# Cutting the first W1 load by contraction tile, issuing the first M and MLP matmuls as separate operations and rewriting every engine's order list, in a fused attention and MLP kernel

## Chip, cores, metric

One core of one Trainium2 chip. The metric is device time in microseconds (us) of the slowest core, here the only one. The profile's span of the same execution is 1.8 us shorter. A change counts as faster or slower at 2 per cent.

## The reference

```python
def _attn_ref(q, k, v):                       # (8, 8, 576, 64) each
    q_s = softmax of q over its last axis
    k_s = softmax of k over the sequence
    kv = einsum('bhsd,bhse->bhde', k_s, v)
    return einsum('bhsd,bhde->bhse', q_s, kv)

def _moe_ref(x, w_in, w_out):                 # (4608, 512), (512, 2048), (2048, 512)
    h = x @ w_in
    g = where(h > 0, h, exp(minimum(h, 0)) - 1)
    return g @ w_out
# the output is _moe_ref(heads of the attention side by side, w_in, w_out)
```

(The two softmaxes are shortened to words.)

## The kernel before

The 4608 tokens go through the MLP in 9 blocks of 512. A block has 8 groups; a group is 8 matmuls of the first layer (two tiles of 128 columns of W1, four contraction tiles each), an ELU on ACT and DVE, and then its share of the second layer's 64 matmuls. The attention is done in units ("pairs") of four heads of one batch, and each pair gives two of the four contraction tiles (of 128 rows) of XT, the MLP's input, for the 576 tokens of its batch; one tile holds two of its heads. Pair 0 gives tiles 0 and 1, with which the MLP starts; pair 1 gives tiles 2 and 3, needed a little later. In what follows, q, k and v are the loaded inputs; qsT is the softmaxed q, transposed; VB is v cast to bf16; "kv" are the matmuls of k with v, whose scaled result stands in MBLK; "M" are the matmuls of MBLK with qsT that give XT; GT is the ELU's output, the second layer's input; PS is PSUM. Each engine's operations follow a list that was written down by number (`ORDER`), and waits on semaphores are derived from what each operation reads and writes.

```python
CH = 9; NU = 16                      # pieces of a unit; units ("pairs" below)

def load_w1(self, g0, g1, half, key, after=()):   # half 0: contraction tiles 0, 1; half 1: 2, 3
    ...
    for h in range(2):               # the two halves of the partitions
        self.S.add("gp", ..., lambda e, h=h: e.dma_start(self.W1[h:128:2, ks, sl], w[h, :, ks, sl]), ...)

def ao_mm(self, n, x, ps, at=0):     # "M": XT of a pair = its block-diagonal M times its qsT
    def mm(e):
        for f in range(2):           # two matmuls, two PSUM banks, one operation
            last = e.matmul(P[:, y:y + n_], M[:, f, :], T[:, c0:c1, f * 64:f * 64 + 64], ...)

def hg_mm(self, j, g, ps, key, half=None):        # first layer, group g of block j
    def mm(e):
        for t in range(2):
            for kc in kcs:           # all four contraction tiles, or two of them
                last = e.matmul(P[:, t * 512:(t + 1) * 512], self.W1[:, kc, ...], self.XT[:, kc, ...], ...)

# start of the program (cut)
for g0, g1, half in ((0, 3, 0), (0, 3, 1), (3, 5, None), (5, 8, None)):
    self.load_w1(g0, g1, half, -30, ...)
...
self.load_w2(0, -29); self.load_w2(1, -29)        # W2 comes in four quarters, between q, k, v of pairs 2 and 3
...
for half in range(2):                             # groups 0 to 2 of block 0
    for g in range(3):
        self.hg_mm(0, g, turns[g], key, half)
for g in range(8):
    self.hg(0, g, turns[g], key, "da"[g % 2], g > 2)
```

The softmax here doesn't subtract the row's maximum and nothing guards it: scores larger than these inputs give would overflow.

Of the kernel before, what the change touches and what calls it, by code (L numbers as in the profile page):

```python
# [21 lines left out]
ISSUE = {"sp": 550, "act": 550, "gp": 740}  # L22
ORDER = {
    "pe": (
        "30 28 32 43 45 47 50 67 54 68 70 71 69 72 82 86 93 115 103 90 129 128 137 136 131 139 107 "
        "130 138 109 151 152 150 126 134 149 132 156 157 158 140 173 146 153 159 172 174 175 233 238 "
        "237 239 192 243 249 245 244 251 250 201 255 257 256 203 263 262 212 268 261 267 269 313 309 "
        "321 317 350 220 325 333 329 280 391 334 282 338 342 291 412 346 351 299 399 404 395 417 362 "
        "400 364 408 425 430 373 413 421 438 426 381 479 434 439 487 450 500 492 483 505 488 452 513 "
        "518 461 496 469 501 526 509 564 514 572 522 538 585 527 540 568 577 573 598 581 586 590 594 "  # L30
        "603 611 549 607 636 599 556 657 640 612 662 644 649 653 645 670 622 666 624 683 688 658 679 "
        "632 675 671 634 696 709 684 692 701 714 697 705 722 727 735 718 710 740 731 748 723 744 761 "
        "736 766 757 753 749 770 787 762 774 779 775 783 788 792 793 805 797 801 809 "),
    "act": (
        "3 22 33 23 24 31 29 34 35 48 44 55 73 76 77 79 83 84 87 94 95 97 104 91 92 116 117 119 98 "
        "108 120 127 135 133 163 160 179 147 166 154 169 205 176 230 231 188 234 180 240 241 191 246 "
        "215 252 253 202 258 204 211 264 213 265 273 270 214 218 310 322 314 217 284 318 221 279 326 "
        "294 355 281 330 296 335 283 290 392 343 297 292 339 293 347 366 352 376 300 405 361 396 378 "
        "363 401 409 365 372 418 375 443 414 454 379 422 374 431 427 382 464 435 449 480 440 451 466 "
        "493 467 484 531 489 453 460 463 506 519 462 497 470 502 542 510 515 565 537 523 539 554 551 "  # L40
        "528 569 578 574 541 552 616 582 591 587 595 548 555 550 608 637 600 626 557 604 641 613 650 "
        "654 621 646 623 663 667 689 631 625 659 680 633 676 672 685 693 715 702 698 635 706 719 728 "
        "711 732 741 724 745 737 767 758 750 771 754 763 776 780 784 789 794 798 806 802 810 812 "),
    "dve": (
        "2 4 5 0 6 7 25 26 37 27 38 39 40 41 42 36 46 49 51 52 53 56 74 75 78 80 81 85 88 89 96 100 "
        "105 106 101 102 122 118 110 111 112 123 124 141 142 143 148 155 182 183 184 177 178 232 206 "
        "235 236 193 194 207 195 196 197 242 208 247 198 248 254 259 260 266 274 275 271 272 276 311 "
        "312 285 319 222 223 286 320 224 225 226 227 287 327 328 356 331 332 357 336 337 358 344 345 "
        "348 349 367 353 368 354 301 369 302 303 304 305 306 397 398 402 403 410 411 444 415 416 445 "
        "446 423 424 428 429 383 384 455 385 386 387 388 436 456 457 437 441 442 485 490 486 532 491 "  # L50
        "498 499 533 471 503 472 534 473 474 504 511 543 544 512 475 476 516 517 524 525 545 529 530 "
        "570 571 575 576 583 584 596 597 617 588 618 589 609 610 601 558 602 619 642 643 559 627 560 "
        "561 562 614 615 628 629 563 655 656 647 648 668 669 660 661 673 674 681 682 686 687 694 695 "
        "707 699 708 700 720 721 712 713 733 734 725 726 746 747 738 739 759 760 751 752 772 764 765 "
        "773 777 778 785 786 "),
    "gp": (
        "1 14 15 16 17 18 19 20 21 57 59 58 63 60 61 62 64 66 99 65 113 125 144 121 114 145 181 186 "
        "189 "),
    "sp": (
        "8 9 10 11 12 13 170 187 161 164 171 185 165 190 200 168 162 199 209 210 216 167 219 277 278 "  # L60
        "229 228 323 315 288 295 316 289 324 298 341 359 308 360 377 307 340 393 370 371 406 394 420 "
        "380 407 419 447 433 390 465 482 432 458 448 389 494 481 495 459 468 478 507 520 535 477 567 "
        "508 521 536 553 566 546 580 547 579 620 605 638 606 593 592 630 651 652 639 677 665 690 664 "
        "678 703 716 717 691 730 704 729 756 768 769 742 755 743 782 781 790 791 795 796 799 800 807 "
        "808 803 804 811 "),
}


# [14 lines left out]
class Sched:  # L83
# [17 lines left out]

    def add(self, eng, dur, emit, key, R=(), W=(), X=(), dma=None, nbytes=0, after=(),
            follow=None, side=0):
# [136 lines left out]
def t_f32r(n):  # L240
    return (n + 32) / 2.4


class Gen:
# [82 lines left out]
            return (self.VR1, "vR1") if n in (1, 3) else (self.VR, "vR0")  # L327
        return self.RAW[n % 2][t], f"{t}R{n % 2}"

    def load_w1(self, g0, g1, half, key, after=()):  # L330
        w = self.w_in.rearrange("(h kc d) f -> h d kc f", h=2, d=D)
        sl = slice(g0 * 256, g1 * 256)
        ks = slice(0, 4) if half is None else slice(2 * half, 2 * half + 2)
        xs = (0, 1) if half is None else (half,)
        for h in range(2):
            self.S.add("gp", ISSUE["gp"], lambda e, h=h: e.dma_start(
                self.W1[h:128:2, ks, sl], w[h, :, ks, sl]), key,
                W=[f"W1_{g}{x}{h}" for x in xs for g in range(g0, g1)],
                dma=f"w1{g0}{xs[0]}{h}", nbytes=(len(xs) * (g1 - g0) << 17) * (1.25 if g0 == 3 else 1), after=after,
                follow=self.gpq)  # L340
            self.gpq = self.S.ops[-1]

    def load_w2(self, s, key, after=()):
        w = self.w_out.rearrange("(jj p) c -> p jj c", p=128)
# [105 lines left out]
    def kv_mm(self, n, ps, at=KV):  # L450
        i = n % 2
        P, ek, VB = self.PS[ps], self.ek(i), self.VB[i]

        def mm(e):
            for c in range(CH):
                for f in range(2):
                    for h in range(2):
                        fs, hs = slice(f * 64, f * 64 + 64), slice(h * 64, h * 64 + 64)
                        x = f * 512 + at
                        last = e.matmul(P[hs, x:x + D + 1], ek[fs, h, c, :],  # L460
                                        VB[fs, h, c, 0:D + 1], start=(c == 0), stop=(c == CH - 1))
            return last
        return 615 if at == self.KV else 290, [f"kR{i}", f"VB{i}", f"VB{i}x", f"VBone{i}"], mm

    def m(self, n, ps, key, at=KV):
        S, i, rz = self.S, n % 2, self.RZK[n % 2]
# [15 lines left out]
    def ao_mm(self, n, x, ps, at=0):  # L482
        i = n % 2
        P, M, T = self.PS[ps], self.MBLK[i], self.qsT[self.alt(n)]
        c0, c1 = self.part(n, x)
        n_ = (c1 - c0) * 64

        def mm(e):
            for f in range(2):
                y = f * 512 + at  # L490
                last = e.matmul(P[:, y:y + n_], M[:, f, :],  # L491
                                T[:, c0:c1, f * 64:f * 64 + 64], start=True, stop=True)
            return last
        return (2 * t_f32r(n_), [f"qsT{self.alt(n)}{y}" for y in (0, 1)] +
                [f"MBLK{i}{y}" for y in ("", 0, 1)], mm)

    def xt(self, n, x, ps, key, eng="act", at=0):
        S = self.S
# [32 lines left out]
            names += [(f"Ox{i}{x}", at, at + 2048) for x in range(2)]  # L531
        return [n for n, lo, hi in names if lo < 4096 * (g + 1) and hi > 4096 * g]

    def hg_mm(self, j, g, ps, key, half=None):
        S = self.S
        P = self.PS[ps]
        banks = [f"b{2 * ps}", f"b{2 * ps + 1}"]
        rc = BLK * (j % 3)
        kcs = range(4) if half is None else range(2 * half, 2 * half + 2)
        xs = [f"X{kc}_{(8 * j + x) % (RING // 64)}" for kc in kcs for x in range(8)]  # L540
        ws = [f"W1_{g}{x}{h}" for x in sorted({kc // 2 for kc in kcs}) for h in range(2)]

        def mm(e):
            for t in range(2):
# [94 lines left out]
    def program(self):  # L639
# [4 lines left out]
        for n, t in ((0, "q"), (1, "q"), (0, "k"), (0, "v"), (1, "k"), (1, "v")):  # L644
            self.load(n, t, -40, "sp", follow=self.gpq)
            self.gpq = S.ops[-1]
            if (n, t) == (0, "k"):
                gate = S.ops[-1]
        loaded = S.ops[-1]
        for g0, g1, half in ((0, 3, 0), (0, 3, 1), (3, 5, None), (5, 8, None)):  # L650
            self.load_w1(g0, g1, half, -30, [gate, self.ident] if half == 0 else ())
            S.ops[-2].behind = loaded
        AB, C, D_ = 3, 2, 1
        self.stage1(0, -8, vconv=CAST0)
# [2 lines left out]
        self.stage1(1, -5, vconv=CAST1)  # L657
        self.m(0, C, -12)
        self.tp(1, D_, -7, ("act", "dve"))
        self.side(C, -5, self.ao_mm(0, 0, C))  # L660
        self.xt(0, 0, C, -10, "both")
        self.side(0, -3, self.kv_mm(1, 0))
        kv1 = S.ops[-1]
        self.m(1, 0, -12)
        S.spare_until = S.ops[-4]
        self.side(0, -2, self.ao_mm(1, 0, 0))
        self.xt(1, 0, 0, -10, "both")
        for o in S.ops:
            if o.eng == "pe":
# [4 lines left out]
            start=True, stop=True)  # L674
# [89 lines left out]

        key = 0
        turns = [3, 1, 2, 0, 3, 1, 0, 2]
        for half in range(2):
            for g in range(3):
                self.hg_mm(0, g, turns[g], key, half)
        for g in range(8):  # L770
            self.hg(0, g, turns[g], key, "da"[g % 2], g > 2)
            if g == 4:
# [50 lines left out]
        i = self.oslot % len(self.OSB)  # L823
# [43 lines left out]
```

## Time and profile before

| | before |
|---|---|
| time, median of 3 runs, later of 6 | 301.47, 301.38 us |
| span of the profiled execution | 299.0 us |
| PE busy | 96% |
| first MLP matmul | 14.95 us |
| last W1 columns landed | 24.71 us |
| last MLP matmul starts | 295.72 us |

PE is the bound, so it is read as one stream. Here are its two main groups of instructions, from the page: line, engine, operation, tiles, shapes and count, then the time busy, the mean ns of one, and the idle time ahead of them.

```profile
L592 PE MATMUL PS<-W,GT 128*128 128x512 f32 (+1 forms) x592 | 141.4, 386 | 0.4 <-DVE GT L582 0.4
L547 PE MATMUL PS<-XT,W 128*128 128x512 f32 x576 | 140.5, 391 | 0.7 <-DVE RZK L469 0.5
```

The two MLP layers have 592 and 576 matmuls and keep PE for 282 of 299 us. The idle time shown is short, but it isn't the whole of what a wait costs: a matmul counts as busy until its modelled end, so a pause shows in full only in the distance between the starts of two matmuls. When nothing waits, that distance is 227 ns. Below I count the 1168 MLP matmuls by their starts and compare the time of the same one in two kernels. This "lag" shows where in the program time is won and lost.

### The profile page before, as it was taken

What the parts mean: (1) busy time and instruction counts of PE and PEld (TensorE: products, weight loads), DVE (VectorE), ACT (ScalarE), POOL (GpSimd) and SP (SyncE); (2) the same over time, 40 slices, a digit from 0 to 9 for tenths busy, and PEclk for the clock granted to TensorE, in tenths of its full rate; (3) what the DMA queues carried; (4) which work ended last, traced back from release to release, by engine and by line L of the source; (5) the groups of instructions that cost most, each with busy time, mean ns of one, the idle gap of its engine ahead of it and who ended that gap; (6) DMA issues with size and microseconds to landing.
All of it is one profiled execution on the core that took longest, in us unless ns stands there. A gap on an engine that the chain in (4) does not pass through costs nothing.

```text
span 299.0 us, 4421 instructions
## 1 busy us (share of the span) xinstructions
PE 287.1 (96%) x1851; PEld 234.5 (78%) x1851; DVE 189.5 (63%) x244; ACT 182.3 (61%) x212; POOL 21.7 (7%) x33
## 2 busy tenths in 40 slices
PE   0899999999999999999999999999999999999995
PEld 0487877677888888888888888888888888888885
DVE  3958935985898685894568855588427256655500
ACT  5858848988977967867755766534462423432411
POOL 0860145100000000000000000000000000000000
PEclk9999999999999999999999999999999999999999
DMA  7999998994498697289546327041312302004214
GB/s 260 387 398 389 390 391 262 240 371 157 118 247 259 141 338 181 71 263 266 175 116 164 88 66 186 2 99 37 86 36 51 70 2 53 0 0 107 64 41 105
DMA packets 35443, 49.96 MB, mean 167 GB/s; under 512 B 16352, under 2 KB 16608, under 8 KB 35424
## 3 DMA queue, kind: packets, MB, share of 16 engines
q1 hardware_dynamic: 29840, 34.15, 41.3%
q0 software_dynamic: 5504, 15.47, 16.3%
q8 instruction: 14, 0.23, 0.3%
q10 hardware_dynamic: 80, 0.07, 0.1%
q14 instruction: 5, 0.04, 0.1%
HBM read 36.70 MB, written 9.44 MB: 154 GB/s over the span
## 4 chain that ended last, share of the span: by engine, by line
PE 89%; DVE 4%; DMA 3%; ACT 1%; SPq 1%; issue 0%
PE PS L592 43%; PE PS L547 41%; PE PS L491 3%; DMA QT<-QS 2%; PE PS L460 2%; DMA QR<-in_q_dram 1%; DVE ZQ L376 1%; DVE QS L384 1%; PE PS L407 1%; SPq L634 1%; DVE XT L516 0%; DVE GT L582 0%; ACT QR L356 0%; ACT qsT L435 0%; ACT ESB L563 0%; DVE MBLK L473 0%
## 5 line engine op out<-in xcount | busy, mean ns | idle before, releaser
L592 PE MATMUL PS<-W,GT 128*128 128x512 f32 (+1 forms) x592 | 141.4, 386 | 0.4 <-DVE GT L582 0.4
L547 PE MATMUL PS<-XT,W 128*128 128x512 f32 x576 | 140.5, 391 | 0.7 <-DVE RZK L469 0.5
L547 PEld LDWEIGHTS PS<-XT,W 128*128 128x128 f32 x576 | 107.1, 188 | 24.0 <-DVE XT L516 0.9
L592 PEld LDWEIGHTS PS<-W,GT 128*128 128x128 f32 x592 | 107.7, 188 | 22.1 <-DVE GT L582 0.8
L563 ACT ACTIVATE ESB<-PS 128x1024 f32<-128x1024 f32 x72 | 73.7, 1027 | 64.7 <-PE PS L547 64.3
L580 DVE TENSOR_SCALAR ESB<-ESB 128x1024 f32<-128x1024 f32 x64 | 44.4, 695 | 67.0 <-ACT ESB L563 66.4
L582 DVE TENSOR_TENSOR GT<-ESB,PS 128x1024 fp32r<-128x1024 f32 x64 | 77.7, 1217 | 1.8
L624 ACT ACTIVATE OSB<-PS 128x512 f32<-128x512 f32 x31 | 18.2, 598 | 30.9 <-PE PS L592 30.6
L376 DVE TENSOR_REDUCE ZQ<-QR 128x18 f32<-128x1152 f32 x16 | 21.5, 1344 | 7.3 <-ACT QR L356 7.2
L513 ACT ACTIVATE XT<-PS 128x512 fp32r<-128x512 f32 (+6 forms) x32 | 19.5, 608 | 7.0 <-PE PS L491 6.5
L384 DVE TENSOR_TENSOR QS<-QR,RZQ 128x1152 f16<-128x1152 f32 x16 | 21.6, 1353 | 0.3
L356 ACT ACTIVATE QR<-QR 128x1152 f32<-128x1152 f32 x16 | 18.6, 1165 | 2.9 <-DMA QR<-in_q_dram 2.9
L360 ACT ACTIVATE KR<-KR 128x1152 bf16<-128x1152 f32 x16 | 18.5, 1160 | 3.0 <-DMA KR<-in_k_dram 3.0
L435 ACT ACTIVATE qsT<-QT 128x1152 fp32r<-128x1152 f16 x12 | 14.0, 1166 | 0.7 <-DMA QT<-QS 0.7
L369 ACT ACTIVATE VB<-VR 128x1152 bf16<-128x1152 f32 (+1 forms) x12 | 13.5, 1124 | 0.7 <-DMA VR<-in_v_dram 0.7
L491 PE MATMUL PS<-qsT,MBLK 128*128 128x320 f32 (+5 forms) x64 | 13.9, 303 | 0.0
L491 PEld LDWEIGHTS PS<-qsT,MBLK 128*128 128x128 f32 x64 | 11.7, 190 | 2.6 <-DVE MBLK L473 0.2
L576 DVE SCALAR_TENSOR_TENSOR GT<-PS,ESB 128x1024 fp32r<-128x1024 f32 x8 | 9.8, 1220 | 4.2 <-ACT ESB L574 4.2
L672 PE MATMUL PS<-ID 128*128 128x512 f16 x7 | 3.3, 590 | 7.5 <-ACT QR L356 7.5
L473 DVE TENSOR_TENSOR MBLK<-PS,RZK 64x128 fp32r<-64x128 f32 x32 | 9.2, 289 | 0.9
L574 ACT ACTIVATE ESB<-ESB 128x1024 f32<-128x1024 f32 x8 | 8.5, 1060 | 0.2
L469 DVE RECIPROCAL RZK<-PS 128x2 f32<-128x2 f32 x16 | 2.6, 164 | 8.7 <-PE PS L460 7.7
(29 smaller groups left out, 59.7 us busy)
## 6 DMA issues: line engine op xcount, KB each, us to landing
out_dram<-OSB SPq DMA_DIRECT2D x62, 128.0 KB, 2.4
QR<-in_q_dram SPq DMA_DIRECT2D x12, 576.0 KB, 5.3
KR<-in_k_dram SPq DMA_DIRECT2D x12, 576.0 KB, 5.6
VR<-in_v_dram SPq DMA_DIRECT2D x12, 576.0 KB, 5.6
W<-in_moe_w_out_dram POOLq DMA_DIRECT2D x4, 1024.0 KB, 18.9
QR<-in_q_dram POOLq DMA_DIRECT2D x4, 576.0 KB, 11.4
KR<-in_k_dram POOLq DMA_DIRECT2D x4, 576.0 KB, 11.6
VR<-in_v_dram POOLq DMA_DIRECT2D x4, 576.0 KB, 8.0
```

The lines of the kernel that those rows point to most:

```text
L356: S.add("act", t_act(1152, False), lambda e: e.activation(flat(q), flat(q), AF.Exp), key - 3, X=[f"qR{i}"], follow=self.table)
L360: S.add("act", t_act(1152, False), lambda e: e.activation(ek[:, :, :, :].rearrange("p h c d -> p (h c d)"), flat(k), AF.Exp), key - 2, X=[ ...
L376: S.add("dve", t_dve(1152), lambda e: e.tensor_reduce(self.ZQ[i][:, :, :].rearrange("p h c -> p (h c)"), q[:, :, :, :].rearrange("p h c d ...
L384: S.add("dve", t_dve(1152), lambda e: e.tensor_tensor(qso, q[:, :, :, :], rz, ALU.mult), key - 3, R=[f"qR{i}", f"RZQ{i}"], W=[f"QS{self.al ...
L491: last = e.matmul(P[:, y:y + n_], M[:, f, :], T[:, c0:c1, f * 64:f * 64 + 64], start=True, stop=True)
L513: S.add("act", t_act((h1 - h0) * n_, True), lambda e, dst=dst, src=src: e.activation(dst, src, AF.Copy), key, W=W, X=X)
L547: last = e.matmul(P[:, t * 512:(t + 1) * 512], self.W1[:, kc, tt * 128:(tt + 1) * 128], self.XT[:, kc, rc:rc + BLK], start=(kc == 0), stop ...
L563: S.add("act", t_act(1024, True), lambda e: e.activation(esb[:, :], P[:, :], AF.Exp), key, W=[f"E{i}"], X=banks)
L580: S.add("dve", t_dve(1024, 2), lambda e: e.tensor_scalar(esb[:, :], esb[:, :], 1.0, -1.0, ALU.min, ALU.add), key, X=[f"E{i}"])
L582: S.add("dve", t_dve(1024), lambda e: e.tensor_tensor(gt, esb[:, :], P[:, :], ALU.max), key, R=[f"E{i}"], W=gw, X=banks)
L592: last = e.matmul(dst, GT[:, jj, ts * 128:(ts + 1) * 128], self.W2[:, jj, c0:c1], start=(jj == 0), stop=(jj == 15))
L624: S.add("act", t_act(512, True), lambda e: e.activation(osb[:, :], src, AF.Copy), key, W=[f"O{i}0", f"O{i}1"], X=[f"b{bk}"])
```

## The change

The intent is to start the MLP sooner: contraction tile 0 of W1 can land by itself, the XT copy of one half of a pair (two heads, one contraction tile; the texts say "head") doesn't wait for the other half's M, and the MLP's first matmuls need one contraction tile only. All five order lists were written anew for it; they make up most of the diff and are left out here. The numbers 600 (`margin`) and 350 are estimates of the program's own scheduler, which also sets by such estimates how many filler matmuls keep PE busy before the MLP starts.

```diff
@@ -327,18 +328,18 @@
             return (self.VR1, "vR1") if n in (1, 3) else (self.VR, "vR0")
         return self.RAW[n % 2][t], f"{t}R{n % 2}"
 
-    def load_w1(self, g0, g1, half, key, after=()):
+    def load_w1(self, g0, g1, kcs, key, after=()):
         w = self.w_in.rearrange("(h kc d) f -> h d kc f", h=2, d=D)
         sl = slice(g0 * 256, g1 * 256)
-        ks = slice(0, 4) if half is None else slice(2 * half, 2 * half + 2)
-        xs = (0, 1) if half is None else (half,)
+        ks = slice(kcs[0], kcs[-1] + 1)
         for h in range(2):
             self.S.add("gp", ISSUE["gp"], lambda e, h=h: e.dma_start(
                 self.W1[h:128:2, ks, sl], w[h, :, ks, sl]), key,
-                W=[f"W1_{g}{x}{h}" for x in xs for g in range(g0, g1)],
-                dma=f"w1{g0}{xs[0]}{h}", nbytes=(len(xs) * (g1 - g0) << 17) * (1.25 if g0 == 3 else 1), after=after,
+                W=[f"W1_{g}{x}{h}" for x in kcs for g in range(g0, g1)],
+                dma=f"w1{g0}{kcs[0]}{h}", nbytes=(len(kcs) * (g1 - g0) << 16) * (1.25 if g0 == 3 else 1), after=after,
                 follow=self.gpq)
             self.gpq = self.S.ops[-1]
+            self.gpq.margin = 600
 
     def load_w2(self, s, key, after=()):
         w = self.w_out.rearrange("(jj p) c -> p jj c", p=128)
@@ -460,7 +461,7 @@
                         last = e.matmul(P[hs, x:x + D + 1], ek[fs, h, c, :],
                                         VB[fs, h, c, 0:D + 1], start=(c == 0), stop=(c == CH - 1))
             return last
-        return 615 if at == self.KV else 290, [f"kR{i}", f"VB{i}", f"VB{i}x", f"VBone{i}"], mm
+        return 615 if at == self.KV else 350, [f"kR{i}", f"VB{i}", f"VB{i}x", f"VBone{i}"], mm
 
     def m(self, n, ps, key, at=KV):
         S, i, rz = self.S, n % 2, self.RZK[n % 2]
@@ -493,6 +494,18 @@
             return last
         return (2 * t_f32r(n_), [f"qsT{self.alt(n)}{y}" for y in (0, 1)] +
                 [f"MBLK{i}{y}" for y in ("", 0, 1)], mm)
+
+    def ao_parts(self, n, ps, key):
+        i = n % 2
+        P, M, T = self.PS[ps], self.MBLK[i], self.qsT[self.alt(n)]
+        c0, c1 = self.part(n, 0)
+        n_ = (c1 - c0) * 64
+        for f in range(2):
+            self.S.add("pe", t_f32r(n_), lambda e, f=f: e.matmul(
+                P[:, f * 512:f * 512 + n_], M[:, f, :], T[:, c0:c1, f * 64:f * 64 + 64],
+                start=True, stop=True), key,
+                R=[f"qsT{self.alt(n)}{y}" for y in (0, 1)] + [f"MBLK{i}{y}" for y in ("", 0, 1)],
+                X=[f"b{2 * ps + f}"], side=1)
 
     def xt(self, n, x, ps, key, eng="act", at=0):
         S = self.S
@@ -531,14 +544,16 @@
             names += [(f"Ox{i}{x}", at, at + 2048) for x in range(2)]
         return [n for n, lo, hi in names if lo < 4096 * (g + 1) and hi > 4096 * g]
 
-    def hg_mm(self, j, g, ps, key, half=None):
+    def hg_mm(self, j, g, ps, key, half=None, kc=None):
         S = self.S
         P = self.PS[ps]
         banks = [f"b{2 * ps}", f"b{2 * ps + 1}"]
         rc = BLK * (j % 3)
         kcs = range(4) if half is None else range(2 * half, 2 * half + 2)
+        if kc is not None:
+            kcs = (kc,)
         xs = [f"X{kc}_{(8 * j + x) % (RING // 64)}" for kc in kcs for x in range(8)]
-        ws = [f"W1_{g}{x}{h}" for x in sorted({kc // 2 for kc in kcs}) for h in range(2)]
+        ws = [f"W1_{g}{x}{h}" for x in kcs for h in range(2)]
 
         def mm(e):
             for t in range(2):
@@ -647,8 +662,8 @@
             if (n, t) == (0, "k"):
                 gate = S.ops[-1]
         loaded = S.ops[-1]
-        for g0, g1, half in ((0, 3, 0), (0, 3, 1), (3, 5, None), (5, 8, None)):
-            self.load_w1(g0, g1, half, -30, [gate, self.ident] if half == 0 else ())
+        for g0, g1, kcs in ((0, 3, (0,)), (0, 3, (1,)), (0, 3, (2, 3)), (3, 5, range(4)), (5, 8, range(4))):
+            self.load_w1(g0, g1, kcs, -30, [gate, self.ident] if kcs == (0,) else ())
             S.ops[-2].behind = loaded
         AB, C, D_ = 3, 2, 1
         self.stage1(0, -8, vconv=CAST0)
@@ -657,13 +672,13 @@
         self.stage1(1, -5, vconv=CAST1)
         self.m(0, C, -12)
         self.tp(1, D_, -7, ("act", "dve"))
-        self.side(C, -5, self.ao_mm(0, 0, C))
+        self.ao_parts(0, C, -5)
         self.xt(0, 0, C, -10, "both")
         self.side(0, -3, self.kv_mm(1, 0))
         kv1 = S.ops[-1]
         self.m(1, 0, -12)
         S.spare_until = S.ops[-4]
-        self.side(0, -2, self.ao_mm(1, 0, 0))
+        self.ao_parts(1, 0, -2)
         self.xt(1, 0, 0, -10, "both")
         for o in S.ops:
             if o.eng == "pe":
@@ -764,9 +779,9 @@
 
         key = 0
         turns = [3, 1, 2, 0, 3, 1, 0, 2]
-        for half in range(2):
+        for kc in range(4):
             for g in range(3):
-                self.hg_mm(0, g, turns[g], key, half)
+                self.hg_mm(0, g, turns[g], key, kc=kc)
         for g in range(8):
             self.hg(0, g, turns[g], key, "da"[g % 2], g > 2)
             if g == 4:
```

(cut: the hunk with the lists `ORDER`; besides the renumbering, they move operations on every engine and through the whole program.)

## The prediction

> **What bounds the kernel now.** I read the page first, then the chain of work that ended last (first 40 us), the timeline in narrow windows from 10 to 18 us, the waits of each engine, the landing of each early transfer, and last the places where PE paused.
>
> ```profile
> span 299.0 us, 4421 instructions
> PE 287.1 (96%) x1851; PEld 234.5 (78%) x1851; DVE 189.5 (63%) x244; ACT 182.3 (61%) x212; POOL 21.7 (7%) x33
> PE   0899999999999999999999999999999999999995
> DMA  7999998994498697289546327041312302004214
> ```
>
> PE is busy in every slice but the first two and the last. So a change that adds and removes no matmul can move three things only: when the stream of MLP matmuls starts, pauses inside it, and the tail. The tail is the last stores; their code is not touched. The start, from the chain in order of time (start us, us, what):
>
> ```profile
> 13.59 0.69 DVE qsT L417
> 14.28 0.60 DVE XT L516
> 14.88 0.09 DVE RZK L469
> 14.96 1.16 PE PS L547 x4
> 16.12 0.47 PE PS L491 x2
> 16.58 13.91 PE PS L547 x60
> ```
>
> The first MLP matmul (L547) begins at 14.95 us. It needs both halves of XT of head pair 0 and both contraction tiles of the first W1 piece. The timeline shows what made XT (start, us, engine, line):
>
> ```profile
> 12.95 0.67 ACT L369 ACTIVATE VB<-VR 128x576 bf16<-128x576 f32 x1
> 13.06 0.71 PE L491 MATMUL PS<-qsT,MBLK 128*128 128x512 f32 x2
> ...
> 13.81 0.60 ACT L513 ACTIVATE XT<-PS 128x512 fp32r<-128x512 f32 x1 [0.19 <-PE PS L491]
> ...
> 14.20 0.68 DVE L516 CAST XT<-PS 128x512 fp32r<-128x512 f32 x1
> 14.30 0.70 ACT L414 ACTIVATE qsT<-PS 128x640 fp32r<-128x640 f16 x1
> ```
>
> ACT's half is ready at 14.41, DVE's at 14.88. The transfer is just as late: taking the W1 issues one by one, the first starts at 8.41 and lands 5.2 us later (13.6), the second starts at 9.15 and lands 5.7 us later (14.86). Both hold contraction tiles 0 and 1, one half of the partitions each. So two independent things end within 0.02 us of each other.
>
> The last W1 piece is a second gate. It is issued at 12.84 and lands 11.9 us later, at 24.7. The weight load of group 5 waits for just that (timeline, window 24.4 to 25.2):
>
> ```profile
> 24.07 1.42 PE L547 MATMUL PS<-XT,W 128*128 128x512 f32 x5
> ...
> 24.75 0.53 PEld L547 LDWEIGHTS PS<-XT,W 128*128 128x128 f32 x3 [0.26 <-DMA W<-in_moe_w_in_dram]
> ```
>
> Starts of 512-wide matmuls are 227 ns apart when nothing waits; the second matmul of this group came 337 ns after the first, so this wait costs about 0.11 us. Later I looked for starts further apart than that: the largest cluster is at 54 to 56 us, where the first second-layer matmuls of block 1 wait for the GT of the group just before them:
>
> ```profile
> 54.98 0.76 PEld L592 LDWEIGHTS PS<-W,GT 128*128 128x128 f32 x4 [0.81 <-DVE GT L582]
> 54.98 1.23 DVE L576 SCALAR_TENSOR_TENSOR GT<-PS,ESB 128x1024 fp32r<-128x1024 f32 x1
> 54.98 1.19 PE L592 MATMUL PS<-W,GT 128*128 128x512 f32 x4 [0.39 <-DVE GT L582]
> ```
>
> There the starts are 773, 335, 478 and 340 ns apart: over 227 that is 0.55 + 0.11 + 0.25 + 0.11 = 1.0 us. Two smaller pauses are at 65.2 us (0.26 + 0.11) and 74.0 us (0.16 + 0.11).
>
> **What the Trainium skill says.** "DMA: Bandwidth & Descriptors", Why a DMA increments its semaphore by 16 and not by 1: only the full 16 means that all data has landed. The trace agrees and shows the price: of the last W1 piece, most engines' updates are in by 22.7 us, the last at 24.71. Same page, Anatomy of one DMA: an estimate of 2.0 us fixed plus bytes over 436 GB/s per transfer. Here the fixed part is hidden, as transfers queue: landings of 384 KB pieces on most engines are 0.97 us apart, 405 GB/s, so cutting one in two should cost little bandwidth. "PSUM — Partial Sum Buffer", PSUM bank collisions raise a hardware error: PE writing and another engine reading must be kept apart by bank. That is why one operation over both banks makes ACT wait for both matmuls; the trace agrees, the ACT copy starting at 13.81 when the second matmul ends at 13.77.
>
> **The change, part by part.**
>
> *W1.* The first load goes from 4 issues of 384 KB to 4 of 192 KB and 2 of 384 KB: the same bytes, the same 3 KB runs. Two more issues of 0.63 us each put POOL's later issues back by about 1.3 us. The last W1 issue is then at about 14.1, still over 10 us ahead of its landing: no cost, since bandwidth (about 390 GB/s from 4 us on) and not issue sets the landing. Contraction tile 0 has the bytes of the one transfer that landed at 13.6, so it should land about there instead of 14.86; tile 1 about 14.9; the last piece at 24.7 to 24.9.
>
> *M matmuls apart.* Each half of XT can be copied 0.23 to 0.31 us sooner, if its engine is free. DVE is not (pair 1's qsT copy ends at 14.28). ACT is not either, because the written order changes too: ACT now does exp of K of pair 1, then the 640-wide qsT copy (0.70), then the half of VB (0.67), and only then XT of pair 0. Step by step: the exp starts at about 12.0 (0.1 later, as the first transpose group now has five in place of four), the qsT copy at 13.1, VB at 13.7, XT at 14.3, ready at 14.95. The kv matmuls of pair 1 can't run before that VB (14.4 to 14.9) and stand ahead of the MLP on PE. So the first MLP matmul comes at about 15.0: no gain, +0.05. What the new order buys is that pair 1's qsT is early, which was not what was waited for.
>
> *MLP by contraction tile.* PE now does three pairs (groups 0 and 1 tile 0, group 0 tile 1), 6 x 0.23 = 1.4 us, then M of pair 1 at 16.4. Its MBLK is ready at about 15.8 (15.60 before, kv 0.4 later). XT of pair 1 is needed after four more matmuls at 17.7 and is ready at 17.4 and 17.7. No pause worth a count. Group 5 would be reached after 42 matmuls: 15.0 + 42 x 0.228 = 24.6, so it meets the same landing of 24.7. Whatever the start gains or loses within 0.1 us is lost or given back here. Sum to this point: 0 to +0.1 us.
>
> *The new order of everything else.* The lists in the diff, with the new operations' numbers taken out, differ in many places. Group 6 now comes ahead of group 7 in block 0: it needs PS0, freed by group 3's GT at 26.5, when PE wants it at 26.7: fits. q of pairs 2 and 3 are now loaded before the second W2 quarter, which then lands at 31.65 + 1.5 = 33.15 and is wanted after 12 matmuls from 30.7, at 33.4: fits by 0.25 us. In block 1 group 1 now goes first and group 3's 8 matmuls (1.8 us) stand between group 2 and the second layer's first matmuls. That fills the pause at 54 to 56 us, worth up to 1.0 us. But group 3 needs the PSUM of group 1, whose way out is exp 1.03, relu 1.06 and DVE 1.22, with an output copy of 0.6 between: 3.9 us and hops, against 20 matmuls x 0.227 = 4.5 us. I count half, -0.5 us.
>
> Sum: +0.1 - 0.5 = -0.4 us, 301.47 - 0.4 = 301.1 us.
>
> **Rivals.** (1) The start is really won: tile 0 lands 1.3 us sooner, and if XT were ready by 14.2 the stream would start 0.7 us sooner. For it: separate banks and smaller pieces are made for that. Against it: ACT's written order, and the gate at 24.7, which takes back all but its 0.11 us unless that piece also lands sooner. With the 54 us pause gone as well: 300.3 us. (2) The transfers get worse: two more of them, W1 on the critical path at 24.7, W2 with 0.25 us to spare, each landing set by the slowest engine. If each lands 0.3 us later and no pause goes: 302 us. (3) The pause at 54 us only moves to another bank wait, or a new one comes: 301.5 us, "nothing happened". For it: 0.5 us of slack at group 3 is thin, and DVE and ACT are at 60 per cent with bursts.
>
> **Range and chances.** All ways lie within 1 us of the time before, against 6 us for 2 per cent, and the three runs before spread by 0.7 us. I take 300.4 to 301.9 us. Faster by over 2 per cent would take more pauses than PE has (some 12 us idle, 7 us of it the first wait for data and 3 us the tail): 0.005. Slower by over 2 per cent would need a stall in each block: 0.01.
>
> **What would show it.** Right: first L547 between 14.8 and 15.2; the qsT copy of pair 1 ahead of XT on ACT; a weight load waiting for W1 near 24.8; no 0.5 us pause near 54 us. Wrong: a start below 14.5 with group 5 not waiting for W1 (rival 1); W1 or W2 landing after 25.0 or 33.5 with PE pausing there (rival 2); new pauses above 0.3 us between 30 and 80 us (rival 3).

## The result

| | before | after |
|---|---|---|
| time, median of 6 runs | 301.38 us (301.1 to 301.81) | 301.17 us (300.94 to 302.35) |
| span of the profiled execution | 299.0 us | 299.4 us |
| first MLP matmul | 14.95 us | 14.76 us |
| first two W1 transfers landed | 13.59, 14.86 us | 13.20, 13.69 us |
| last W1 columns landed; group 5 starts | 24.71; 24.75 us | 24.80; 24.84 us |
| last MLP matmul starts | 295.72 us | 296.04 us |

The ratio is 1.0002, 95% interval 0.9983 to 1.002. A ratio here is the mean time of one kernel's fast runs over that of the other's of the same rounds, so it is not quite the ratio of the medians in the table. In five later rounds (e11) it was 1.0016 (1.0003 to 1.003). The change is "the same".

The page of the changed kernel, the lines that answer to those of before:

```profile
span 299.4 us, 4428 instructions
...
PE 287.2 (96%) x1854; PEld 233.9 (78%) x1854; DVE 189.8 (63%) x244; ACT 182.1 (61%) x212; POOL 23.1 (8%) x35
...
L607 PE MATMUL PS<-W,GT 128*128 128x512 f32 (+1 forms) x592 | 140.9, 385 | 0.7 <-DMA W<-in_moe_w_out_dram 0.7
L562 PE MATMUL PS<-XT,W 128*128 128x512 f32 x576 | 140.9, 392 | 0.2 <-DVE GT L597 0.2
```

L607 and L562 are the lines 592 and 547 of before. The idle time has changed owner: the wait of the second layer for DVE's GT is gone, and a wait of the second layer for W2 (`in_moe_w_out`) has come.

The lag of the changed kernel, in us, at the same MLP matmul:

| MLP matmul | before starts at | lag | what lies between |
|---|---|---|---|
| 1st | 14.95 | -0.19 | |
| 41st (group 5) | 24.75 | +0.09 | waits for W1 at groups 3 and 5 |
| 89th | 36.75 | +0.32 | groups 6 and M wait for PSUM |
| 151st | 53.98 | +1.19 | wait for the last quarter of W2 |
| 161st | 57.31 | +0.12 | the pause of before at 54 us is not there |
| 201st | 68.30 | +0.47 | waits of 0.1 us each at 60 us, at M (65 us) and for DVE's GT (66 us) |
| last | 295.72 | +0.32 | |

So the front wins 0.19 us and gives back 0.28, block 0's second half loses 0.23 and 0.87, block 1 wins 1.07, loses 0.35, and the rest of the program wins 0.15 (a wait for DVE's GT at 74 us is shorter). A change with many parts ends where it began because a win and a loss of 0.9 to 1.1 us each stand against each other. Every lag is that of one execution against one execution of the kernel before; the experiments ran on several chips, and only the ratios compare runs side by side on one.

The start, in the timeline of the changed kernel (start, us, engine, line, operation):

```profile
12.94 0.71 ACT L415 ACTIVATE qsT<-PS 128x640 fp32r<-128x640 f16 x1
...
13.53 0.69 ACT L370 ACTIVATE VB<-VR 128x576 bf16<-128x576 f32 x1
14.10 0.61 ACT L526 ACTIVATE XT<-PS 128x512 fp32r<-128x512 f32 x1
...
14.27 0.49 PE L461 MATMUL PS<-VB,KR 64*64 64x65 bf16 x36 [0.26 <-ACT VB L370]
...
14.76 1.66 PE L562 MATMUL PS<-XT,W 128*128 128x512 f32 x6
```

As predicted, ACT's order puts the qsT copy and VB ahead of XT; XT of the first half is ready at 14.71 and the MLP starts 0.05 us later, although its W1 tile has been there since 13.69. (The kv matmuls of pair 1, which had waited for VB, keep PE until just then; both hang on ACT's list.) The second gate is met just as before (timeline at 24 us), and after it two waits for PSUM that DVE has to free, at group 6 and at M of pairs 0 and 1:

```profile
24.84 1.70 PEld L562 LDWEIGHTS PS<-XT,W 128*128 128x128 f32 x8 [0.26 <-DMA W<-in_moe_w_in_dram]
...
26.77 1.67 PEld L562 LDWEIGHTS PS<-XT,W 128*128 128x128 f32 x8 [0.23 <-DVE GT L591]
...
28.62 0.52 PEld L492 LDWEIGHTS PS<-qsT,MBLK 128*128 128x128 f32 x4 [0.19 <-DVE GT L597]
```

At 54 us, where the kernel before pauses, the matmuls now run through (timeline):

```profile
54.27 3.11 PE L562 MATMUL PS<-XT,W 128*128 128x512 f32 x13
...
55.07 0.76 DVE L595 TENSOR_SCALAR ESB<-ESB 128x1024 f32<-128x1024 f32 x1
```

And the new pause, which nothing in the kernel before answers to (timeline at 44 us):

```profile
43.67 0.49 PE L461 MATMUL PS<-VB,KR 64*64 64x65 bf16 x36
...
44.90 0.30 PEld L607 LDWEIGHTS PS<-W,GT 128*128 128x128 f32 x2 [0.86 <-DMA W<-in_moe_w_out_dram]
44.90 0.50 PE L607 MATMUL PS<-W,GT 128*128 128x512 f32 x1 [0.75 <-DMA W<-in_moe_w_out_dram]
```

The last quarter of W2 lands at 44.86 us. In the kernel before it landed at 43.03, ahead of v of pair 3 at 44.54; the new list of loads has v of pair 3 first (41.95) and W2 last. Both kernels load the same bytes at about the same rate (387 to 398 GB/s in the slices from 7 to 45 us before, 371 to 394 after), so one of the two has to come later.

### The profile page after: what moved, and what is told of

It reads as the page before. It is cut to its first block, busy times and chain, and to the rows that moved or that the text cites. A ratio compares the mean times of both kernels' runs of the same rounds, so it can differ in the third digit from the quotient of the medians.

```text
span 299.4 us, 4428 instructions
## 1 busy us (share of the span) xinstructions
PE 287.2 (96%) x1854; PEld 233.9 (78%) x1854; DVE 189.8 (63%) x244; ACT 182.1 (61%) x212; POOL 23.1 (8%) x35
## 4 chain that ended last, share of the span: by engine, by line
PE 80%; DMA 10%; POOL 4%; DVE 3%; ACT 1%; issue 0%; SPq 0%
PE PS L607 40%; PE PS L562 37%; DMA W<-in_moe_w_out_dram 8%; PE PS L492 2%; DMA KR<-in_k_dram 2%; POOL W L336 2%; PE PS L461 1%; DVE GT L597 1%; POOL W L347 1%; ACT ESB L578 1%; ACT KR L361 1%; POOL QR L320 0%; POOL KR L320 0%; DVE QS L385 0%; POOL VR L320 0%; DVE ESB L595 0%
## 5 line engine op out<-in xcount | busy, mean ns | idle before, releaser
L607 PE MATMUL PS<-W,GT 128*128 128x512 f32 (+1 forms) x592 | 140.9, 385 | 0.7 <-DMA W<-in_moe_w_out_dram 0.7
L562 PE MATMUL PS<-XT,W 128*128 128x512 f32 x576 | 140.9, 392 | 0.2 <-DVE GT L597 0.2
L562 PEld LDWEIGHTS PS<-XT,W 128*128 128x128 f32 x576 | 106.8, 188 | 23.7 <-DVE GT L597 0.9
L607 PEld LDWEIGHTS PS<-W,GT 128*128 128x128 f32 x592 | 108.0, 188 | 22.1 <-DMA W<-in_moe_w_out_dram 0.9
L492 PEld LDWEIGHTS PS<-qsT,MBLK 128*128 128x128 f32 x60 | 10.9, 189 | 3.1 <-DVE MBLK L474 0.5
L492 PE MATMUL PS<-qsT,MBLK 128*128 128x320 f32 (+4 forms) x60 | 12.9, 299 | 0.0
L687 PEld LDWEIGHTS PS<-ID 128*128 128x128 f16 x10 | 1.0, 116 | 8.8 <-ACT QR L357 7.4
```

The costliest lines, as they stand in the source:

```text
L607: last = e.matmul(dst, GT[:, jj, ts * 128:(ts + 1) * 128], self.W2[:, jj, c0:c1], start=(jj == 0), stop=(jj == 15))
```

## The experiments

My theory after the result had three parts. (A) The front's win is taken back by a second gate, the landing of the last W1 columns. (B) The pause at 54 us is taken out by the new order. (C) It is paid for at 44 us by waiting for W2. The rivals are named in each expectation. "e1" to "e12" are runs.

### e2: the front alone

The change's operations, loads and order up to group 5, then the list of the kernel before.

```diff
 ORDER: every engine
-  changed kernel's list
+  changed kernel's list up to group 5 of block 0, then the list of before, renumbered
```

> The change's operations, its W1 pieces and its order up to group 5 of block 0 (about 25 us), then the order of the kernel before. Theory (what the front wins is taken back where groups 3 and 5 wait for their W1 columns to land): first MLP matmul at 14.76 us as in the changed kernel, 0.19 us before the kernel before; at the 42nd MLP matmul (group 5) 0.0 to 0.15 us behind it; pause at 54 us there again (about 1.0 us), none at 44 us; span 299.0 to 299.3 us. Rival (the front is worth its 0.19 us or more, and only the later order spoils it): span 298.8 us or less.

Measured: first MLP matmul at 14.78, group 5 at 24.84 with the landing at 24.80, pauses of 773 and 462 ns at 54.3 and 55.9 us as before, none at 44 us; span 298.9; ratio 0.9989 (0.9964 to 1.0013). The lag is -0.17 at the 1st matmul, +0.09 at the 41st, -0.13 at the last. That is what (A) asks for at the gate. The span sits between the two theories, by 0.1 us of each, and the times can't tell them apart.

### e4 and e8: a start that is really sooner, with and without the second gate

e4 puts ACT's list at the start back to XT first:

```diff
 act list, start (numbers of the changed kernel)
-3 24 35 25 26 31 33 36 46 37 51 59
+3 24 35 25 26 33 31 36 37 51 46 59
 pe list, start
-30 32
+32 30
```

> The changed kernel with ACT's order at the start as in the kernel before: the half of VB of pair 1 and XT of pair 0 ahead of the qsT copy of pair 1. Theory (landing of W1 is a second gate): first MLP matmul at 14.2 to 14.4 us instead of 14.76, so the start does win 0.4 to 0.5 us; group 3 then waits until 21.05 and group 5 until 24.8, and from the 42nd MLP matmul on the kernel stands where the changed kernel does, within 0.1 us; span 299.2 to 299.6. Rival (the start is what counts, the landing follows): span 0.4 us or more below the changed kernel's 299.4.

e8 is e4 with groups 3 to 7 of block 0 reading columns of W1 that have long landed (the result is wrong):

```diff
+        wg = g % 3 if j == 0 else g
-                tt = 2 * g + t
+                tt = 2 * wg + t
```

(cut: the wait for W1 follows the same index)

> The kernel of e4 (XT ahead of the qsT copy), wrong on purpose: groups 3 to 7 of block 0 use the W1 columns of groups 0 to 2, which have landed. Theory (landing of W1 is the second gate): first MLP matmul at 14.1 to 14.3 us as in e4, no wait at groups 3 and 5, so group 5 starts 42 matmuls later at 23.7 to 23.9 instead of 24.4 to 24.8; the win of 0.6 to 1.0 us at the 42nd MLP matmul against the changed kernel. By the 150th MLP matmul it is taken back by the landing of W2 (last quarter at about 44.5), so span still 299.0 to 299.4. Rival (PSUM or ACT holds group 5 anyway): group 5 no sooner than 24.3.

Timeline of e4, at the start and at group 5:

```profile
14.13 1.09 PE L564 MATMUL PS<-XT,W 128*128 128x512 f32 x3
...
24.47 0.30 PEld L564 LDWEIGHTS PS<-XT,W 128*128 128x128 f32 x2 [0.78 <-DMA W<-in_moe_w_in_dram]
24.47 0.50 PE L564 MATMUL PS<-XT,W 128*128 128x512 f32 x1 [0.36 <-DMA W<-in_moe_w_in_dram]
```

e4 starts 0.63 us before the changed kernel, so ACT's order had been holding the start. (The swap of pair 0's two transposes, which is also in the diff, moves ACT's next operation by 0.03 us only.) At group 5 it waits. My number for group 5 (where the changed kernel is, within 0.1 us) was missed: it was 0.37 us ahead there, since in this execution the last W1 columns landed at 24.43 instead of 24.80, which is 0.37 as well. So group 5 follows the landing, not the start: in the profiles of before, after, e2, e4, e6 and e7 it begins 0.04 us after the landing each time, for landings from 24.26 to 24.87. It is a gate only where the stream comes first: in e3 and e5, which have the changed kernel's start, the columns landed at 24.17 and 24.26, and group 5 began at 24.71 and 24.58 without a wait. In e8, where the columns don't matter, group 5 began at 24.25, which is 0.57 us ahead of the landing in that execution (24.82); I had expected 23.7 to 23.9, but its start was at 14.32 and three waits of 0.11 us came on the way. e8's win was gone at the 151st matmul (lag +0.95, W2 at 44.62), as expected, and its last MLP matmul came at +0.04. Ratios: e4 1.0018 (0.9984 to 1.0051), e8 0.9983 (0.9956 to 1.001). (A) holds where that landing is late; the rival of e4 (the start is what counts, span 0.4 us or more below) falls, with a span 0.24 us below, as does, by 0.05 us, the rival of e8 (PSUM holds group 5 until 24.3).

### e6 and e7: each half of the front alone

e6 is the kernel before with W1 in pieces; e7 is the kernel before with the operations apart, their order as it was.

```diff
 e6: load_w1 by contraction tiles as in the change; hg_mm, ao_mm and order as before
 e7: ao_parts and hg_mm by kc as in the change; load_w1 and order as before
```

> The kernel before with only the first W1 load cut in pieces, its matmul operations and order unchanged. Theory: contraction tile 0 lands at 13.6 to 13.8 us, but the first MLP operation needs tiles 0 and 1 and both halves of XT, so it starts at 14.9 to 15.0 as before; the last W1 columns land within 0.2 us of before (24.7); span 298.9 to 299.3. Rival (more transfers cost bandwidth): last W1 columns land at 25.0 or later, span up by the same.

> The kernel before with only the operations taken apart (M per head of the pair, MLP by contraction tile), W1 loads and order unchanged. Theory: XT of the first head on ACT starts when VB is cast, at 13.55 instead of 13.81; the first MLP matmul still waits for the second W1 transfer, which holds half the partitions of tile 0, at 14.86, so it starts at 14.85 to 14.95; span 298.9 to 299.2. Rival (the operations are what wins the start): first MLP matmul at 14.4 or earlier.

e6: start 14.99, last W1 at 24.87, span 299.4, ratio 0.9999 (0.9973 to 1.0026). Cutting the load does nothing by itself, and the last landing moved by 0.16 us, which is less than it moves between executions. e7 surprised: start 14.48, span 298.7, ratio 0.9972 (0.9945 to 0.9999) in one round. But its second W1 transfer landed at 14.44 in that execution, 0.43 us sooner than in the profile of before, and its last at 24.26, 0.45 sooner; its lag is -0.45 at the 41st matmul and -0.37 at the end.

### e10: e7 in more rounds

> The kernel of e7 once more, in more rounds. Theory (its 0.4 us were one execution in which the second and the last W1 transfer landed 0.43 and 0.45 us sooner than in the profile of the kernel before, and in an execution with the later landing it stands where the kernel before does): ratio 0.9985 to 1.000, and the start of the first MLP matmul follows the landing of the second W1 transfer within 0.1 us when that is after 14.4 us. Rival (taking the operations apart is worth 0.4 us by itself): ratio 0.998 or less with an interval below 1, and a start at 14.5 with the second transfer landing at 14.8 or later.

Ratio 0.9987 (0.9975 to 1.000). This lies in my theory's band, but 0.13 per cent of 301 us is 0.4 us, the rival's size, so the ratio doesn't tell the two apart; the rival's own signs (0.998 or less, a start at 14.5 with the transfer at 14.8) didn't come. The theory's detail missed too: the start was 14.77, 0.16 us after the second transfer had landed (14.61). In this execution the kv matmuls of pair 1 came last, behind a filler matmul that keeps PE busy; in e7 it was the transfer. Timelines of e7 (first fence) and e10 (second):

```profile
13.87 0.48 PE L463 MATMUL PS<-VB,KR 64*64 64x65 bf16 x36 [0.16 <-ACT VB L372]
...
14.48 0.56 PEld L564 LDWEIGHTS PS<-XT,W 128*128 128x128 f32 x3 [0.24 <-DMA W<-in_moe_w_in_dram]
```

```profile
14.36 0.48 PE L463 MATMUL PS<-VB,KR 64*64 64x65 bf16 x36
...
14.77 0.30 PEld L564 LDWEIGHTS PS<-XT,W 128*128 128x128 f32 x2
```

Taking the operations apart moves the start up to the next of three things that end within 0.5 us of each other: the second W1 transfer, the copies of XT, and kv of pair 1. e10 puts its worth at 0.13 per cent, with an interval from 0.25 per cent to nothing. In both profiles later waits took back part of what had been won: the lag goes from -0.71 at the 201st matmul to -0.37 at the last in e7 (DVE's GT at 74 us), and from -0.48 to +0.20 in e10 (0.79 us between two starts at 71 us, behind an ACT copy of qsT).

### e3: no wait for the last quarter of W2

```diff
+        sl = (lambda jj: jj - 12 if jb == 0 and jj >= 12 else jj)
-                last = e.matmul(dst, GT[:, jj, ...], self.W2[:, jj, c0:c1], ...)
+                last = e.matmul(dst, GT[:, jj, ...], self.W2[:, sl(jj), c0:c1], ...)
```

(cut: the wait for W2 follows the same index)

> The changed kernel, wrong on purpose: in block 0 the last quarter of the second layer uses the first quarter of W2, which landed long before. Theory (the pause at 44 us is the last quarter of W2, landing at 44.86 us, behind one load more than before): the 942 ns between two matmuls at 44 us goes, worth 0.7 to 0.85 us, and most of it stays won to the end: span 298.6 to 298.8 us against 299.4. Rival (the pause is covered by another wait, so that the time comes back within block 1): span above 299.1 us.

The 942 ns went: the lag against the kernel before is +0.23 at the 151st matmul instead of +1.19. But the span was 299.2, which is the rival's, and the last matmul is only 0.26 us sooner than in the changed kernel; ratio 1.0001 (0.9968 to 1.0033). Waits within block 1 gave 0.7 us back: 616 ns between two starts at 56 us and 412 at 59.5. How the first came about shows in the timeline at 54 to 57 us:

```profile
53.87 1.15 POOL L375 CAST VB<-VR 128x1152 bf16<-128x1152 f32 x1 [4.33 <-DMA VR<-in_v_dram]
54.11 1.45 DVE L597 TENSOR_SCALAR ESB<-ESB 128x1024 f32<-128x1024 f32 x1
...
55.60 1.22 DVE L599 TENSOR_TENSOR GT<-ESB,PS 128x1024 fp32r<-128x1024 f32 x1
...
56.87 1.65 PE L611 MATMUL PS<-W,GT 128*128 128x512 f32 x6 [0.23 <-DVE GT L599]
```

DVE's `tensor_scalar`, 0.69 us elsewhere, took 1.45. It had started while GpSimd's cast of VB was running. The Trainium skill, "SBUF — State Buffer", Who interferes with whom, says that GpSimd and a DVE `tensor_scalar` in its two-port mode take one pair of ports as an exclusive lock, and whoever comes second waits for the whole instruction. The trace agrees that it is held up until the cast is over: here, in e4 and in the changed kernel, the `tensor_scalar` ended 0.54 us after the cast's end (55.56 after 55.02, 55.50 after 54.96, 55.83 after 55.29), wherever it had begun. That is 0.15 us less than it takes alone, so by these traces a part of it isn't held up. In the changed kernel the pause at 44 us made DVE late, so that it met only the end of the cast (0.76 us): the new pause was hiding this one.

### e5: the cast later

e3, and the cast made to start after that `tensor_scalar`:

```diff
-                          R=[vname], W=[f"VB{i}{x}"])
+                          R=[vname], W=[f"VB{i}{x}"],
+                          after=[S.ops[187]] if (eng, n) == ("gp", 5) else ())
```

> The kernel of e3 (no wait for the last quarter of W2, wrong on purpose), and in it GpSimd's cast of VB of pair 5 made to start only after DVE's first tensor_scalar of block 1. Theory (what took back the 0.97 us of e3 is one DVE tensor_scalar that took 1.45 us instead of 0.69, since GpSimd's cast ran at the same time, and DVE has no slack from 48 to 57 us): that tensor_scalar takes 0.7 us, the 616 ns between matmuls at 56 us goes and the 412 ns at 59.5 us shrinks; lag against the changed kernel at the 200th MLP matmul -0.7 us or more, span 298.5 to 298.8 us. Rival (DVE and ACT are simply full there and any order of them gives the same time): tensor_scalar short, but the pause stays elsewhere before 66 us, span 299.1 or more.

Timeline of e5:

```profile
53.99 0.70 DVE L598 TENSOR_SCALAR ESB<-ESB 128x1024 f32<-128x1024 f32 x1
...
54.76 1.15 POOL L375 CAST VB<-VR 128x1152 bf16<-128x1152 f32 x1 [5.28 <-DVE ESB L598]
```

The 616 ns pause at 56 us and the 412 ns at 59.5 us both went; the lag against the kernel before is -0.67 at the 201st matmul, which is 1.14 us ahead of the changed kernel, and -0.69 at the last. Span 298.4, ratio 0.9968 (0.9951 to 0.9985). This settles (B) and (C): the changed order wins 1.06 us at 54 us (lag +0.10 at the 151st, -0.96 at the 161st) and gives back 0.29 up to the 201st, the wait for W2 costs about as much as it wins, and behind that wait stood a second one. e5 computes a wrong result, since the true last quarter of W2 can't be had at that time. So it is not a version to keep.

### e1, e9 and e12: the new order of block 1 with the old order of loads

If the loads of before have no pause at 44 us, and the new order none at 54, can one have both? e1 joins the lists of before up to 47 us with the lists of after from there.

```diff
 ORDER: every engine, numbers of the kernel before
+  list of before up to kv of pair 3, M and group 0 and 1 of block 1, then the changed kernel's list
```

> The kernel before with its own operations and its own order up to about 47 us, and from there the changed kernel's order. Theory (the changed order takes about 1.0 us of pauses out at 54 to 57 us, and gives them back at 44 us, where it waits for the last quarter of W2): no wait for W2 at 44 us, first MLP matmul at 14.95 us as before, no pause over 0.3 us between 53 and 58 us, span 0.9 to 1.2 us below the kernel before's 299.0 (297.8 to 298.1), ratio about 0.9965. Rival (the pauses only move, PSUM banks set the pace in block 1 whatever the order): span within 0.3 us of before.

It took 309.45 us, ratio 1.0271 (1.0243 to 1.0299). Both theories missed, because of my cut:

```profile
78.80 1.23 DVE L579 SCALAR_TENSOR_TENSOR GT<-PS,ESB 128x1024 fp32r<-128x1024 f32 x1 [7.51 <-DMA out_dram<-OSBX]
...
80.08 1.22 PE L595 MATMUL PS<-W,GT 128*128 128x512 f32 x2 [5.33 <-DVE GT L579]
```

GT of block 1 lies over the buffers from which block 0's outputs are stored. One of those stores stood in SyncE's list behind a load that, in the new ACT order, is released late; it was issued at 74.85 us. A second wait, of 0.9 us at 48 us, came from kv of pair 3 standing right ahead of its M. Lists of five engines belong together. e9 mends this (SyncE's new list as a whole, kv of pair 3 further ahead of its M) and takes e7's operations:

> A correct kernel made of the parts that seemed to pay: operations apart as in e7 with the W1 loads and the order of the kernel before up to the end of block 0 (W2 ahead of v of pair 3), then block 1 and later in the changed kernel's order, with the cuts of e1 mended (kv of pair 3 one MLP operation earlier ahead of its M, SyncE's stores in the changed order). Theory: no wait for W2 at 44 us, no 0.5 us pause at 54 us, no tensor_scalar of DVE over 0.75 us between 45 and 60 us; lag at the 200th MLP matmul against the kernel before -0.6 to -1.1 us, span 298.0 to 298.5 us, ratio about 0.997. Rival (block 1 has no slack on DVE with kv of pair 3 this late): pause of 0.3 us or more at 54 to 60 us again, span 298.7 to 299.2.

Ratio 1.0004 (0.999 to 1.0019): no gain. Its profiled execution with a span of 740 us (at a granted clock of 1.00, so what slowed it is not shown) says nothing of this; e12 is the same kernel.

> The kernel of e9 once more, since its profile fell in an execution[...] (span 740 us), to see where its gain went. Theory (DVE and ACT have no slack in block 1, and with kv of pair 3 at 47 us DVE starts its work there late): DVE busy over 0.9 of 50 to 58 us, no wait for W2 at 44 us, but PE pauses on DVE's GT between 53 and 61 us of 0.4 us or more in sum; the lag against the kernel before at the 200th MLP matmul is -0.4 to +0.1 us. Rival (a cut of mine made a new wait elsewhere, as in e1): a pause of 0.4 us or more whose releaser is not DVE, or one after 66 us that the changed kernel does not have.

Span 300.1, ratio 1.0018 (0.9985 to 1.0051). At the 13th matmul the lag was already +0.60: the fourth W1 transfer landed at 17.90 in this execution (16.80 in the profile of before), and no MLP matmul started between 17.06 and 17.99. In block 1 the new order won 0.60 us where it takes the pause out, having lost 0.54 between the 129th and 151st matmul, and lost 0.57 more up to the 201st. From the busy time by stretches of e12:

```profile
50.00:54.00 4.00, 3.88 (x17) 2.75 (x16) 3.90 (x5) 3.75 (x6) 0.85 (x2) 1.00 0.87 286
54.00:58.00 4.00, 3.84 (x18) 2.71 (x17) 3.74 (x5) 3.79 (x5) 1.15 (x1) 1.00 1.04 213
```

The columns are PE, PEld, DVE, ACT and POOL busy us, then clock, DMA share and GB/s. DVE is busy 7.6 of 8 us and ACT 7.5; but in the kernel before it is 7.7 and 7.8 there, so the busy share alone doesn't single e12 out. The waits do: 553 ns between two starts at 55.8 us and 403 at 60.7, both for DVE's GT, and ahead of them one for ACT's copy of XT:

```profile
50.70 0.30 PEld L564 LDWEIGHTS PS<-XT,W 128*128 128x128 f32 x2 [0.56 <-ACT XT L528]
```

That copy belongs to pair 3, whose kv stands in the list at 47 us, behind v, which in this order of loads lands last (44.55, cast until 45.76). So the theory for e12 is borne out in kind, and so is its rival's first sign (a pause of 0.4 us or more whose releaser is not DVE: this one, and the one at 17 us); the lag at the 201st matmul (+0.99) was beyond my range, and the W1 landing (0.67 us up to the 13th) explains only part of that.

### e11: the change again

> The changed kernel as it is, beside e9 and e10 on one chip. Theory: ratio 0.999 to 1.001, wait for W2 at 44 us (0.6 to 0.9 us), no pause over 0.3 us between 53 and 58 us, and the start of group 5 within 0.1 us of the landing of the last W1 transfer. Rival (the change is a small gain that six runs hid): ratio below 0.9985.

Ratio 1.0016 (1.0003 to 1.003), just above the band that I had given. The profiled execution was slow (granted TensorE clock 0.664, span 414.8 us), so the other three expectations are not answered by this run; the first profile answers them.

## Why the prediction was right

Class and range were right: 301.17 us against a predicted 301.1 in 300.4 to 301.9. But the sum was right partly by luck: the win at 54 us was 0.6 us larger than counted, and a wait of 0.9 us at 44 us was not in the sum; these two errors cancel. And the 0.2 us between the medians is no more than noise, with the ratio at 1.0002. By its steps:

1. **The start, +0.05: -0.19 measured.** The mechanism was right (ACT's list holds XT; e4 undid it and won 0.63 us). The term was 0.24 us too long, 0.13 of it because I let ACT's operations follow each other end to start; in the trace the next one starts up to 0.13 us before the last one's end (13.53 against 12.94 + 0.71). The rest is when ACT's exp of K of pair 1 began, at 11.89 in place of my 12.0, and that differs between executions: in e2, e5 and e3, whose code and order are the same up to there, it began at 11.91, 11.98 and 12.17 and the MLP at 14.78, 14.85 and 15.04, 2.87 us later each time, as here. So three of these four starts lie before the 14.95 of the kernel before and one behind it, and the -0.19 is one execution's.
2. **The gate at 24.7, 0 to +0.1 up to group 5: +0.09 measured**, with the landing at 24.80 in the predicted 24.7 to 24.9. e4 and e8 showed the gate; e3 and e5 show executions without it.
3. **Group 6 ahead of group 7, "fits": it didn't quite.** Two waits for PSUM cost 0.23 us together with what follows.
4. **The second W2 quarter, "fits by 0.25 us": right** (landed at 33.23, no wait). I stopped there. **The failed step is that I didn't check the last quarter**: further down the same list v of pair 3 now comes ahead of it. It cost 0.87 us of lag. The rival "the transfers get worse" had the mechanism in a general form, not this transfer.
5. **The pause at 54 us, half of 1.0 us: all of it went (1.07 us).** The slack that I called thin was enough. Of that, 0.35 us came back by the 201st matmul, which I hadn't counted.
6. **Rival 3, a new pause, is what happened**, with a number close to its 301.5: a pause above 0.3 us at 44 us, within the window that I had named. The signs of being right came too, but for the start, 0.04 us before its window.

What stays open: whether the operations taken apart are worth anything by themselves (0 to 0.25 per cent, e10), and why the same W1 transfers land up to 0.9 us apart in executions of kernels whose loads are the same or nearly so.

## What to carry to other kernels

When loads run without a break at the start of a kernel (here at about 390 GB/s until 45 us), the stream behind them can meet a gate at each landing; a sooner start is kept only if every later gate that it meets moves too, so list all landings with the time at which each is wanted, to the last one. A pause can hide another: take it out alone and see what comes up before calling it the cost. An order of loads that serves one consumer makes another wait, and lists of several engines can't be cut and joined one by one.

## What the Trainium skill lacked or had wrong

- "DMA: Bandwidth & Descriptors", Latency and other measured facts, calls two engines "usually slower" without a number or its spread. Here the last of the 16 updates of the last W1 transfer came 1.35 us after the one before it in the kernel before and 0.07 us in e12, and in twelve profiles the transfer landed between 24.01 and 24.87 us. Where the stream waits for this transfer, group 5 moves with it, 0.04 us behind. Which engine was last is not shown.
- "TensorE: Matmul & The Clock Gate", Back-to-back issue gap, gives about 131 ns per matmul of 512 columns in a stream and about 216 ns isolated, without naming float32r. In this kernel's stream of float32r matmuls, each with its own weights, starts are 227 ns apart, nearer to the second figure.
- No page that I read says what a wait costs beyond itself: after most waits of the two profiles the second matmul starts 335 to 342 ns after the first, 0.11 us more than in the stream (337 ns at 24.75 us before, 338 at 44.90 after; 313 at the first MLP matmul of before).
- "SBUF — State Buffer", Who interferes with whom, is right and has no number for this pairing: a `tensor_scalar` of 0.69 us ended 0.54 us after the end of GpSimd's 1.15 us cast, and took up to 1.45 us.
